# Landmark attention, gated MLP and Mish MLP: the fused weight product moved to the front, w1 and w2 reloaded as fp32, landmark evictions twice as wide

## The chip, the core and the metric

The kernel runs on one core of one Trainium2 chip. The metric is the device time in microseconds (us). Five engines work side by side, each through its own list of instructions in order: TensorE (PE; its weight loads are shown as PEld), VectorE (DVE), ScalarE (ACT), GpSimd (POOL), and SyncE (SP), which here only issues DMAs. Semaphores make an engine wait for another.

## The reference

Landmark attention (32 landmarks, 6 steps of an iterative inverse) feeds a gated MLP without activation between its weights, and that feeds an MLP with Mish:

```
q_lm, k_lm = means of q and k over 18 tokens       # batch 4, 8 heads, 576 tokens, head 64
A = softmax(q k_lm^T); Bm = softmax(q_lm k_lm^T); C = softmax(q_lm k^T)
Z = Bm^T / (norms of Bm); 6 times: Z = 2Z - Z Bm Z
x = A Z C v                                        # 2304 tokens x 512
h = (x w1) * (x w2);  y = h w3 w_out               # w1, w2: 512 x 1024
out = (g w_out2), g = mish(y w_in)                 # w_in: 512 x 2048
```

All weights arrive as float64; q, k and v as fp32.

## The kernel before

**Decoding.** A weight unit is 128 x 512 float64 numbers, 512 KB. `ld` (SP) loads it, `da` (ACT or DVE, `top_bits`) takes the top bits, and `db` (DVE, `join`, L214) joins them with the rest into fp32. Units `wo0` to `wo7` are w_out of the gated MLP, `w30` to `w315` are w3 transposed, `w{bp}{s}{x}` are 16 units of w1 and w2, and 32 numbered units are the Mish MLP's weights.

**Stages.** (1) `mm n x` multiplies w3 by w_out once for all tokens, since no activation stands between them: 64 fp32 products, which PE runs as 128 instructions (L344). (2) Attention for batches 0 to 3 (names with the batch last): sums over 18 tokens, scores, softmaxes, the inverse's six steps (`nm`, `nu`), and a landmark matrix `LT`. `A` is not multiplied out: it stays as two halves high and low (`ahi`, `alo`) of the operand `AT`. (3) `m b s` multiplies LT of a batch by w1 and w2 (L784, 8 fp32 products, which PE runs as 16 instructions). The result is evicted from PSUM as a high part (`mh`, ACT) and a low part (`ml`, DVE, `less`, L223) into one of three slots `M`. `xa` and `xb` multiply AT by a slot for w1 and w2, six products each (a pair of high and low parts takes three: L194 to L196); `xc` (ACT) and `xm` (DVE) make the gated product, `sh` and `sl` split it. (4) `y` multiplies it by the result of (1). (5) The Mish MLP runs in 24 steps, each of products `Z` and then `O`; the first of its products, `Z0 0`, ends what the text calls the first part of the program.

Batches 0 and 1 take w1 and w2 in a first pass (`bp` 0), 2 and 3 in a second (`bp` 1); before the change each pass loads and decodes all 16 units.

**What sets the order.** Each step is recorded with its engine, what it must follow and which buffers it takes. The table `ORDER` then says in what order the steps are issued; `issue` goes through it and hands out buffers from pools as their last readers pass. So an engine's list is the table's, and a table entry such as `da w34@ACT` also sets the engine. Twenty products of a tile of ones (`SPIN`) run on PE before the first step.

PSUM has eight banks, all in one pool `w`. An `m` takes two of them, one for each of two head groups, and is evicted in four pieces of 128 x 256 a kind.

Of the kernel before, what the change touches and what calls it, by code (L numbers as in the profile page):

```python
# [223 lines left out]

# [1231 lines left out]
```

## Time and profile before

| | |
|---|---|
| time, 3 runs | 717.61 us (717.41 to 718.4) |
| profiled execution, its own time | 719.34 us |
| its span, first to last instruction | 717.5 us |
| busy: PE, DVE, ACT, POOL | 702.5, 419.1, 287.3, 11.2 us |
| instructions on PE (products) | 5004 |
| bytes moved by DMA | 141.38 MB, mean 197 GB/s |
| chain that ended last | PE 94%, DMA 2%, DVE 2%, ACT 1% |

The profiled execution took 719.34 us, 1.73 us more than the median of the runs. Busy time is the time in which an engine had an instruction under way. Matmuls are pipelined, so that their busy times overlap and are longer than what each adds: 302 ns busy for one of 128 x 288 where one starts every 132 ns. The work that a stretch holds is therefore counted in starts and not in busy time. `PEclk` is the clock that TensorE was granted, 1.00 for 2.4 GHz and 0.50 for 1.2 GHz.

### The profile page before, as it was taken

What the parts mean: (1) busy time and instruction counts of PE and PEld (TensorE: products, weight loads), DVE (VectorE), ACT (ScalarE), POOL (GpSimd) and SP (SyncE); (2) the same over time, 40 slices, a digit from 0 to 9 for tenths busy, and PEclk for the clock granted to TensorE, in tenths of its full rate; (3) what the DMA queues carried; (4) which work ended last, traced back from release to release, by engine and by line L of the source; (5) the groups of instructions that cost most, each with busy time, mean ns of one, the idle gap of its engine ahead of it and who ended that gap; (6) DMA issues with size and microseconds to landing.
All of it is one profiled execution on the core that took longest, in us unless ns stands there. A gap on an engine that the chain in (4) does not pass through costs nothing.

```text
span 717.5 us, 12433 instructions
## 1 busy us (share of the span) xinstructions
PE 702.5 (98%) x5004; PEld 597.5 (83%) x5004; DVE 419.1 (58%) x904; ACT 287.3 (40%) x649; POOL 11.2 (2%) x13
## 2 busy tenths in 40 slices
...
GB/s 337 318 289 242 240 206 248 108 194 148 60 89 89 90 134 219 146 207 252 315 65 220 221 350 194 291 232 248 272 211 209 163 205 206 180 219 208 171 1 88
DMA packets 33914, 141.38 MB, mean 197 GB/s; under 512 B 3392, under 2 KB 3776, under 8 KB 30272
## 3 DMA queue, kind: packets, MB, share of 16 engines
...
HBM read 110.69 MB, written 29.88 MB: 196 GB/s over the span
## 4 chain that ended last, share of the span: by engine, by line
PE 94%; DMA 2%; DVE 2%; ACT 1%; issue 0%; SPq 0%; ACTq 0%; DVEq 0%
PE ps L194 27%; PE ps L195 27%; PE ps L196 27%; PE ps L344 7%; PE ps L784 2%; DMA raw<-in_wts_dram 2%; PE ps L405 1%; PE ps L597 1%; DMA q<-in_qT_dram 1%; PE ps L531 1%; PE ps L510 0%; DVE e L420 0%; DVE cmx L481 0%; DVE mx L426 0%; DVE ea L463 0%
## 5 line engine op out<-in xcount | busy, mean ns | idle before, releaser
L195 PE MATMUL ps<-hs,W 128*128 128x288 f32 (+1 forms) x298 | 92.3, 310 | 0.0
L194 PE MATMUL ps<-hs,W 128*128 128x288 f32 (+1 forms) x298 | 92.3, 310 | 0.0
L196 PE MATMUL ps<-hs,W 128*128 128x288 f32 (+1 forms) x298 | 92.2, 309 | 0.0
L1254 DVE TENSOR_TENSOR hsb<-ps,zt 128x384 f32<-128x384 f32 x72 | 39.7, 556 | 88.7 <-PE ps L196 88.2
L1250 ACT ACTIVATE hsb<-hsb 128x768 f32<-128x768 f32 (+1 forms) x48 | 32.8, 684 | 117.4 <-DVE hsb L1254 117.4
L194 PE MATMUL ps<-AT,M 128*128 128x288 f32 x256 | 77.4, 302 | 0.0
L196 PE MATMUL ps<-AT,M 128*128 128x288 f32 x256 | 75.5, 295 | 0.0
L195 PE MATMUL ps<-AT,M 128*128 128x288 f32 x256 | 75.4, 294 | 0.0
L1254 DVE TENSOR_TENSOR zt<-ps,zt 128x384 f32<-128x384 f32 x48 | 26.7, 556 | 83.1 <-PE ps L196 81.0
L344 PE MATMUL ps<-wo,raw 128*128 128x512 f32 x128 | 60.6, 616 | 1.3 <-DVE wo L214 1.3
L194 PEld LDWEIGHTS ps<-hs,W 128*128 128x128 f32 x298 | 56.0, 188 | 2.1 <-ACT M L218 0.8
L196 PEld LDWEIGHTS ps<-hs,W 128*128 128x128 f32 x298 | 55.9, 188 | 1.8
L195 PEld LDWEIGHTS ps<-hs,W 128*128 128x128 f32 x298 | 56.1, 188 | 1.3
L223 DVE TENSOR_TENSOR W<-hsb,W 128x384 fp32r<-128x384 f32 (+1 forms) x72 | 48.8, 686 | 9.6 <-ACT W L1251 9.5
L194 PEld LDWEIGHTS ps<-AT,M 128*128 128x128 f32 x256 | 48.0, 188 | 5.1 <-issue 2.6
L195 PEld LDWEIGHTS ps<-AT,M 128*128 128x128 f32 x256 | 48.1, 188 | 0.5 <-issue 0.5
L196 PEld LDWEIGHTS ps<-AT,M 128*128 128x128 f32 x256 | 48.0, 188 | 0.0
L344 PEld LDWEIGHTS ps<-wo,raw 128*128 128x128 f32 x128 | 24.3, 200 | 26.4 <-issue 21.1
L218 ACT ACTIVATE a<-ps 128x288 f32<-128x288 f32 x64 | 25.5, 411 | 50.9 <-PE ps L196 46.3
L202 ACT ACTIVATE top<-raw 128x512 f16<-128x512 bf16 x48 | 37.3, 785 | 8.8 <-DMA raw<-in_wts_dram 6.2
L195 PE MATMUL ps<-yH,zw 128*128 128x384 f32 x120 | 40.3, 336 | 0.1
L195 PE MATMUL ps<-yH,hs 128*128 128x384 f32 x120 | 40.2, 335 | 0.0
...
## 6 DMA issues: line engine op xcount, KB each, us to landing
...
```

Source lines behind the costliest of these rows:

```text
L194: T.matmul(out=o, lhsT=lh, rhs=rh, start=first, stop=False, skip_group_check=partial)
L195: T.matmul(out=o, lhsT=lh, rhs=rl, start=False, stop=False, skip_group_check=partial)
L196: T.matmul(out=o, lhsT=ll, rhs=rh, start=False, stop=last, skip_group_check=partial)
L202: S.activation(o, i, ACTF.Copy)
L218: S.activation(o, x, ACTF.Copy)
L223: (G if e == "POOL" else V).tensor_tensor(o, x, f32(hi), op=ALU.subtract)
L344: T.matmul(out=got(f"acc{i}"), lhsT=f32(middle(got(f"w3{n}"))[:, o:o + 128]), rhs=WO0[j // 4][:, j % 4], start=j == 0, stop=j == 7)
L405: T.matmul(out=mine(f"{key}{g}{hf}")[32 * i:32 * i + 32, 0:HALF], lhsT=st[lm][r, p, :], rhs=st[x][r, p, hf * HALF:(hf + 1) * HALF], start= ...
L531: T.matmul(out=pc[32 * i:32 * i + 32, :], lhsT=et[0:w, ck, 32 * i:32 * i + 32], rhs=VT[0:w, ck, h * D:(h + 1) * D], start=(ck == 0), stop= ...
L784: T.matmul(out=got(f"p{c}{key}")[32 * i:32 * i + 32], lhsT=LT[r, b, 2 * c + par, :], rhs=w12(f"w{bp}{s}{2 * c + par}")[r], start=True, sto ...
L1250: S.activation(e, src_, ACTF.Mish)
L1254: V.tensor_tensor(o, x, y, op=ALU.add)
```

## The change

Nothing of PE's arithmetic changes: both kernels have 4258 products in their tables' order (5004 as the trace counts them). What changes:

1. **Order.** `ORDER` is a new table. It begins with the units of w_out and w3 and their products; q and k of batch 0 are loaded behind eight weight units, and attention stands between the products.
2. **w1 and w2** are decoded once, stored to DRAM as fp32 (`wsm`, 256 KB each) and loaded from there for the second pass. 16 loads of 512 KB and 16 decodes go; 16 stores and 16 loads of 256 KB come. Both make 8.4 MB.
3. **Evictions of `m`.** Two of the eight PSUM banks become one tile `PAIR` of two banks. Attention of batches 0 and 1 uses them first (pool `v`), then every `m` uses `PAIR` (pool `m2`, one entry), and after the last `m` they return to `w` as two banks. An `m` is now evicted in two pieces of 128 x 512 a kind, where it was four of 128 x 256.
4. **Small operations of attention** move: the softmax of `Bm` takes its shift, exponent and sum in ACT instructions, some additions go to ACT, and POOL takes the subtraction of the row maximum (`asb`, 7 of 8) and the low half of `AT` (`alo`, 6 of 8).

```diff
 ORDER = (
-    "lk0 0,lq0 0,lq1 0,ks3 0,qs3 0,qs4 0,lk1 0,cs0 0,ks4 0,cm00 0,cs1 0,cm10 0,lk0 1,bs 0,cm20 0,cex00 0,ks3 1,"
+    "ld wo0,da wo0@ACT,db wo0,ld w34,da w34@DVE,ld w30,da w30@ACT,db w34,db w30,mm 0 1,ld wo1,da wo1@DVE,db wo1,"
...
-    bank = [ps.tile([128, 512], F32, name=f"ps{i}") for i in range(8)]
+    bank = [ps.tile([128, 512], F32, name=f"ps{i}") for i in range(6)]
+    PAIR = ps.tile([128, 2, 512], F32, name="pair")
+    bank += [PAIR[:, 0], PAIR[:, 1]]
...
-    pools["w"] = bank[0:8]
+    pools["w"], pools["v"], pools["m2"] = bank[0:6], bank[6:8], []
...
-            add(f"asb{g}", "DVE", [f"amx{g}"], a_sub(g))
+            add(f"asb{g}", ("DVE", "POOL"), [f"amx{g}"], a_sub(g))
...
-            add(f"alo{g}", "DVE", [f"ahi{g}"], a_out(g, 1), (), (), [f"ea{g}"])
+            add(f"alo{g}", ("DVE", "POOL"), [f"ahi{g}"], a_out(g, 1), (), (), [f"ea{g}"])
...
+        if bp:
+            step(f"ld {u}", "SP", [f"wsm {d}"], lambda e: nc.sync.dma_start(out=w12(u), in_=WMD[d * 128:(d + 1) * 128, :]),
+                 {"f" + u: "w12"})
+            return
         decode(u, 24 + 4 * s + x, lambda: got(u), {u: "raw"}, lambda: w12(u), ([], {"f" + u: "w12"}, [u]))
+        step(f"wsm {d}", "SP", [f"db {u}"], lambda e: nc.sync.dma_start(out=WMD[d * 128:(d + 1) * 128, :], in_=w12(u)), (), ["f" + u])
...
-                p, m = got(f"p{c}{key}")[:, 256 * x:256 * x + 256], mslot(b, 2 * s + x)
+                p, m = got("p" + key)[:, :, 256 * x:256 * x + 256], mslot(b, 2 * s + x)
                 if i == 0:
-                    copy(e, m[:, 0, c], p)
+                    copy(e, m[:, 0], p)
                 else:
-                    less(e, m[:, 1, c], p, m[:, 0, c])
+                    less(e, m[:, 1], p, m[:, 0])
...
-            for c in range(2):
-                step(f"mh{c} {n}", "ACT", [key, f"mt {n}"], ev(0, c, x))
-                step(f"ml{c} {n}", "DVE", [f"mh{c} {n}"], ev(1, c, x), (), [f"p{c}{key}"])
+            step(f"mh {n}", "ACT", [key] + vacated, ev(0, x), {f"M {n}": "M"})
+            step(f"ml {n}", "DVE", [f"mh {n}"], ev(1, x), (), ["p" + key])
```

SP's list at the start of the program, before and then after (`raw` is the landing place of a weight unit, `k` and `q` are halves of a batch):

```order
L257 DMA idn<-in_ident_dram 128x128
L381 DMA k<-in_kT_dram 128x2x576
L381 DMA q<-in_qT_dram 128x2x576 x2
L381 DMA k<-in_kT_dram 128x2x576
L381 DMA k_72<-in_kT_dram 128x2x576 x2
L210 DMA raw_73<-in_wts_dram 128x2048
L381 DMA q_71<-in_qT_dram 128x2x576 x2
L210 DMA raw_73<-in_wts_dram 128x2048
```

```order
L260 DMA idn<-in_ident_dram 128x128
L202 DMA raw_73<-in_wts_dram 128x2048 x3
L202 DMA raw<-in_wts_dram 128x2048 x4
L202 DMA raw_73<-in_wts_dram 128x2048
L384 DMA k<-in_kT_dram 128x2x576 x2
L384 DMA q<-in_qT_dram 128x2x576 x2
L202 DMA raw_73<-in_wts_dram 128x2048 x3
```

Eight weight units now stand ahead of batch 0's q and k, where six halves of q and k stood ahead of the first unit.

PE's list around `m 0 2` and the first product that reads it (`xa 0 4 0`, the last row after); before, `m 0 2` ends with ps_77 and ps_82, and the rows with ps_79 and ps_83 are `m 1 2`, behind which 16 score products stand:

```order
L784 MATMUL ps_77<-w_669,LT 32x512
L784 MATMUL ps_82<-w_669,LT 32x512
L784 MATMUL ps_79<-w_669,LT 32x512
L784 MATMUL ps_83<-w_805,LT 32x512
L784 MATMUL ps_79<-w_669,LT 32x512
L784 MATMUL ps_83<-w_805,LT 32x512
```

```order
L793 MATMUL pair<-w_370,LT 32x512 x8
L534 MATMUL ps_78<-vt,et 32x64 x20
L186 MATMUL ps_80<-AT_69,M 128x288
L187 MATMUL ps_80<-AT_69,M 128x288
L188 MATMUL ps_80<-AT_69,M 128x288
L186 MATMUL ps_80<-AT_69,M 128x288
L187 MATMUL ps_80<-AT_69,M 128x288
L188 MATMUL ps_80<-AT_69,M 128x288
L186 MATMUL ps_79<-AT_68,M 128x288
```

The two `m` of a pair of batches no longer follow each other, and between `m 0 2` and its first reader stand 20 products of probabilities with v (40 as the trace counts) and one block `xb`.

POOL's list from its start, before (where five more like the last row follow, and nothing else) and after (`e` is a half of A's softmax, `ea` the same turned back):

```order
L1372 MEMSET top 128x1024
L457 ISA
L457 TENSOR_TENSOR e_94<-e_94,sm 128x576
L457 TENSOR_TENSOR e_93<-e_93,sm 128x576
L457 TENSOR_TENSOR e_94<-e_94,sm 128x576
```

```order
L1384 MEMSET top 128x1024
L221 ISA
L221 TENSOR_TENSOR e_92<-e_92,mx 128x576
L221 TENSOR_TENSOR cc<-nm 128x2
L460 TENSOR_TENSOR e_92<-e_92,sm 128x576
L460 TENSOR_TENSOR e_93<-e_93,sm 128x576
L224 TENSOR_TENSOR AT_68<-ea_94,AT_68 128x576
L224 TENSOR_TENSOR AT_68<-ea_95,AT_68 128x576
L221 TENSOR_TENSOR e_93<-e_93,mx 128x576
L221 TENSOR_TENSOR e_92<-e_92,mx 128x576
```

POOL has 20 long operations instead of 8, and each kind of them reads two tiles in SBUF.

## Rows read from the trace of the kernel before

**Rows 1.** Stretches of 10 us: PE, PEld, DVE, ACT, POOL busy (x instructions), clock, DMA share, GB/s

```profile
10.00:20.00 10.00, 6.44 (x100) 2.58 (x101) 9.41 (x25) 3.29 (x9) 0.00 (x0) 0.57 1.04 394
...
60.00:70.00 10.00, 10.00 (x66) 4.07 (x65) 9.85 (x24) 7.51 (x22) 0.00 (x0) 1.00 0.76 267
```

**Rows 2.** Timeline of PE: start, length, engine, line, operation, [idle before, releaser]

```profile
1.45 6.01 PE L1376 MATMUL ps<-ones 128*128 128x512 bf16 x20 [1.45 <-DVE ones L1374]
...
18.66 0.44 PE L597 MATMUL ps<-bt 32*32 32x32 f32 x16 [2.03 <-DVE bt L592]
...
26.76 1.13 PE L344 MATMUL ps<-wo,raw 128*128 128x512 f32 x2 [1.31 <-DVE wo L214]
...
64.61 1.95 PE L784 MATMUL ps<-w,LT 64*32 64x512 f32 x32
...
336.38 0.34 PE L194 MATMUL ps<-yW,zw 128*128 128x384 f32 x1
```

**Rows 3.** The chain that ended last, several stretches: start, length, engine, line, instructions

```profile
51.87 0.83 PE ps L531 x40
52.95 0.36 PE ps L597 x16
...
64.68 1.88 PE ps L784 x32
66.56 7.07 PE ps L344 x16
...
103.18 0.97 PE ps L405 x32
...
134.20 0.44 PE ps L510 x4
134.64 0.11 PE ps L512
```

**Rows 4.** A stretch of 40 us that holds only L194 to L196

```profile
290.00:330.00 40.00, 40.00 (x303) 40.00 (x302) 30.92 (x68) 24.32 (x57) 0.00 (x0) 1.00 0.46 168
```

**Rows 5.** Timeline of DVE at the start

```profile
5.61 1.35 DVE L393 TENSOR_REDUCE sumk<-k 128x64 f32<-128x1152 f32 x1 [4.21 <-DMA k<-in_kT_dram]
...
8.63 1.35 DVE L393 TENSOR_REDUCE sumq<-q 128x64 f32<-128x1152 f32 x1 [0.15 <-DMA q<-in_qT_dram]
```

**Rows 6.** Groups of ACT and DVE by form: xcount, busy, mean ns, idle before

```profile
L202 ACT ACTIVATE top<-raw 128x512 f16<-128x512 bf16 x48 | 37.3, 785 | 8.8 <-DMA raw<-in_wts_dram 6.2 <-DVE wo L214 2.4
L214 DVE SCALAR_TENSOR_TENSOR wo<-raw,top 128x512 int32<-128x512 int32 x8 | 5.5, 683 | 0.2
```

**Rows 7.** A microsecond while PE was busy at the low clock

```profile
33.00:34.00 1.00, 1.00 (x2) 0.34 (x1) 1.00 (x3) 1.00 (x5) 0.00 (x0) 0.50 0.62 158
```

**Rows 8.** DVE's busy time until the first product of m

```profile
5.61:64.61 59.00, 50.59 (x685) 23.64 (x683) 55.85 (x140) 24.79 (x64) 5.09 (x4) 0.86 0.87 316
```

**Rows 9.** Timelines of POOL and of DVE under it

```profile
37.80 1.61 POOL L457 TENSOR_TENSOR e<-e,sm 128x576 f32<-128x576 f32 x1 [36.12 <-DVE sm L452]
...
49.67 1.16 POOL L457 TENSOR_TENSOR e<-e,sm 128x576 f32<-128x576 f32 x1 [8.22 <-ACT et L521]
...
38.80 1.16 DVE L214 SCALAR_TENSOR_TENSOR raw<-raw,top 128x512 int32<-128x512 int32 x1
...
50.17 0.69 DVE L447 TENSOR_SCALAR sm<-sm 128x18 f32<-128x18 f32 x1
```

**Rows 10.** Evictions by form, ACT and DVE

```profile
L218 ACT ACTIVATE W<-ps 128x512 fp32r<-128x512 f32 x8 | 4.8, 603 | 5.4 <-PE ps L344 5.4
L223 DVE TENSOR_TENSOR M<-ps,M 128x256 fp32r<-128x256 f32 x64 | 25.1, 417 | 8.0 <-ACT M L218 6.4 <-PE ps L196 1.1
L223 DVE TENSOR_TENSOR W<-ps,W 128x512 fp32r<-128x512 f32 x8 | 5.4, 688 | 2.5 <-ACT W L218 2.4
```

**Rows 11.** The chain where the Mish stage waited longest

```profile
460.76 0.19 PE ps L196
...
463.68 0.44 PE ps L195
```

More of the change, by code (lines that the diff above doesn't have):

```diff
@@ L220, in copy, with plus, pair @@
             (G if e == "POOL" else V).tensor_scalar(o, x, 1.0, 0.0, op0=ALU.mult, op1=ALU.add)
+    def plus(e, o, x, c):
+        if e == "ACT":
+            S.activation(o, x, ACTF.Copy, bias=c)
+        else:
+            V.tensor_scalar(o, x, c, None, op0=ALU.add)
+    def pair(e, o, x, y, op):
+        (G if e == "POOL" else V).tensor_tensor(o, x, y, op=op)
     def less(e, o, x, hi):
@@ L295, in issue @@
                     free[p].append(i)
-            for key, p in moves.get(n, ()):
-                pools[p].append(got(key))
+            for _, p, x in moves.get(n, ()):
+                pools[p].append(x)
                 free[p].append(len(pools[p]) - 1)
         assert len(done) == len(steps)
-    pools["w"] = bank[0:8]
+    pools["w"], pools["v"], pools["m2"] = bank[0:6], bank[6:8], []
     pools["raw"] = [RAW[:, 1024 * i:1024 * i + 1026] for i in range(4)]
@@ L430, in f @@
             def f(e):
-                V.tensor_tensor(by_token(g), by_token(g), st["mx", g].unsqueeze(2).to_broadcast([128, NT, L]), op=ALU.subtract)
+                pair(e, by_token(g), by_token(g), st["mx", g].unsqueeze(2).to_broadcast([128, NT, L]), ALU.subtract)
             return f
@@ L446, in f @@
             def f(e):
-                V.tensor_scalar(st["sm", g], st["sm", g], 1e-9, None, op0=ALU.add)
+                plus(e, st["sm", g], st["sm", g], 1e-9)
             return f
@@ L564, in b_max, with b_neg, b_exp, b_mul @@
             return f
-        def b_sub(g):
+        def b_neg(e):
+            st["bng"] = sbt([128, 2], "bng", 2)
+            V.tensor_scalar(st["bng"], st["bmx"], -scale / (BLK_T * BLK_T), None, op0=ALU.mult)
+        def b_exp(g):
             def f(e):
                 if g == 0:
-                    st["be"] = sbt([128, 2, L], "be", 2)
-                V.tensor_scalar(st["be"][:, g, :], st["pb"][g], st["bmx"][:, g:g + 1], None, op0=ALU.subtract)
-            return f
-        def b_exp(e):
-            S.activation(st["be"], st["be"], ACTF.Exp, scale=scale / (BLK_T * BLK_T))
-        def b_sum(e):
-            st["bsm"] = sbt([128, 2], "bsm", 2)
-            V.tensor_reduce(st["bsm"], st["be"], axis=AX.X, op=ALU.add)
+                    st["be"], st["bsm"] = sbt([128, 2, L], "be", 2), sbt([128, 2], "bsm", 2)
+                S.activation(st["be"][:, g, :], st["pb"][g], ACTF.Exp, bias=st["bng"][:, g:g + 1],
+                             scale=scale / (BLK_T * BLK_T), accum_out=st["bsm"][:, g:g + 1])
+            return f
         def b_add(e):
-            V.tensor_scalar(st["bsm"], st["bsm"], 1e-9, None, op0=ALU.add)
+            plus(e, st["bsm"], st["bsm"], 1e-9)
         def b_rec(e):
             V.reciprocal(st["bsm"], st["bsm"])
-        def b_mul(e):
-            st["bm"] = sbt([128, 2, L], "bm", 2)
-            V.tensor_tensor(st["bm"], st["be"], st["bsm"].unsqueeze(2).to_broadcast([128, 2, L]), op=ALU.mult)
+        def b_mul(g):
+            def f(e):
+                if g == 0:
+                    st["bm"], st["ns"] = sbt([128, 2, L], "bm", 2), sbt([128, 4], "ns", 2)
+                S.activation(st["bm"][:, g, :], st["be"][:, g, :], ACTF.Copy, scale=st["bsm"][:, g:g + 1],
+                             accum_out=st["ns"][:, g:g + 1])
+            return f
         def b_tr(e):
@@ L603, in b_p0, with n_sum @@
                 tile_mm(st["pp"][:, g, :], st["bt"][:, g, :], st["bt"][:, g, :])
-        def n_sum(i):
-            def f(e):
-                if i == 0:
-                    st["ns"] = sbt([128, 4], "ns", 2)
-                V.tensor_reduce(st["ns"][:, 2 * i:2 * i + 2], st["bt" if i else "bm"], axis=AX.X, op=ALU.add)
-            return f
+        def n_sum(e):
+            V.tensor_reduce(st["ns"][:, 2:4], st["bt"], axis=AX.X, op=ALU.add)
         def n_cp(e):
             st["bc"] = sbt([128, 4, L], "bc", 1)
-            V.tensor_copy(st["bc"], st["ns"].unsqueeze(2).to_broadcast([128, 4, L]))
+            copy(e, st["bc"], st["ns"].unsqueeze(2).to_broadcast([128, 4, L]))
         def n_tr(e):
@@ L625, in n_mul @@
             st["cc"] = sbt([128, 2], "cc", 2)
-            V.tensor_tensor(st["cc"], st["nm"][:, 0:2], st["nm"][:, 2:4], op=ALU.mult)
+            pair(e, st["cc"], st["nm"][:, 0:2], st["nm"][:, 2:4], ALU.mult)
         def n_add(e):
-            V.tensor_scalar(st["cc"], st["cc"], 1e-6, None, op0=ALU.add)
+            plus(e, st["cc"], st["cc"], 1e-6)
         def n_rec(e):
@@ L637, in f @@
                     st["py"] = sbt([128, 2, 2, L], "py", 2)
-                V.tensor_tensor(st["py"][:, :, i, :], st["bm" if i else "pp"],
-                                st["cc"].unsqueeze(2).to_broadcast([128, 2, L]), op=ALU.mult)
+                x = st["bm" if i else "pp"]
+                if e == "ACT":
+                    for g in range(2):
+                        S.activation(st["py"][:, g, i, :], x[:, g, :], ACTF.Copy, scale=st["cc"][:, g:g + 1])
+                else:
+                    V.tensor_tensor(st["py"][:, :, i, :], x, st["cc"].unsqueeze(2).to_broadcast([128, 2, L]), op=ALU.mult)
             return f
@@ L686, in attn @@
         for g in range(2):
-            add(f"bmx{g}", "DVE", ["bs"], b_max(g), old(2, "bsb0", "bsb1"))
+            add(f"bmx{g}", "DVE", ["bs"], b_max(g), old(2, "bng"))
+        add("bng", "DVE", ["bmx0", "bmx1"], b_neg, old(2, "by0", "by1"))
         for g in range(2):
-            add(f"bsb{g}", "DVE", [f"bmx{g}"], b_sub(g), old(2, "bml"), (), [f"pb{g}"])
-        add("by", "ACT", ["bsb0", "bsb1"], b_exp)
-        add("bsm", "DVE", ["by"], b_sum, old(2, "bml"))
-        add("bad", "DVE", ["bsm"], b_add)
+            add(f"by{g}", "ACT", ["bng"] + ["by0"] * g, b_exp(g), old(2, "bml1"), (), [f"pb{g}"])
+        add("bad", ("DVE", "ACT"), ["by0", "by1"], b_add)
         add("brc", "DVE", ["bad"], b_rec)
-        add("bml", "DVE", ["brc"], b_mul, old(2, "npy1", "ns0"))
-        add("btr", "DVE", ["bml"], b_tr, old(2, "ns1", "bp"))
+        for g in range(2):
+            add(f"bml{g}", "ACT", ["brc"] + ["bml0"] * g, b_mul(g), old(2, "npy1", "ns1", "nc"))
+        add("btr", "DVE", ["bml0", "bml1"], b_tr, old(2, "ns1", "bp"))
         add("bp", "PE", ["btr"], b_p0, (), {"pp0": "w"})
-        add("ns0", "DVE", ["bml"], n_sum(0), old(2, "nc"))
-        add("ns1", "DVE", ["btr", "ns0"], n_sum(1))
-        add("nc", "DVE", ["ns0", "ns1"], n_cp, old(1, "ntr"))
+        add("ns1", "DVE", ["btr"], n_sum)
+        add("nc", ("DVE", "ACT"), ["bml1", "ns1"], n_cp, old(1, "ntr"))
         add("ntr", "DVE", ["nc"], n_tr, old(1, "nx"))
         add("nx", "DVE", ["ntr"], n_max, old(2, "nml"))
-        add("nml", "DVE", ["nx"], n_mul, old(2, "npy0", "npy1"))
-        add("nad", "DVE", ["nml"], n_add)
+        add("nml", ("DVE", "POOL"), ["nx"], n_mul, old(2, "npy0", "npy1"))
+        add("nad", ("DVE", "ACT"), ["nml"], n_add)
         add("nrc", "DVE", ["nad"], n_rec)
-        add("npy0", "DVE", ["bp", "nrc"], b_py(0), old(2, "lt0", "lt1"), (), ["pp0"])
-        add("npy1", "DVE", ["nrc", "bml", "npy0"], b_py(1))
+        add("npy0", ("DVE", "ACT"), ["bp", "nrc"], b_py(0), old(2, "lt0", "lt1"), (), ["pp0"])
+        add("npy1", ("DVE", "ACT"), ["nrc", "bml1", "npy0"], b_py(1))
         for k in range(6):
@@ L716, in attn @@
         for hf in range(2):
-            add(f"as{hf}", "PE", [ks, "lq1"], a_scores(hf), (), {f"sc{g}{hf}": "w" for g in range(2)})
+            add(f"as{hf}", "PE", [ks, "lq1"], a_scores(hf), (), {f"sc{g}{hf}": "w" if hf or b > 1 else "v" for g in range(2)})
         for hf in range(2):
@@ L722, in attn @@
             add(f"amx{g}", "DVE", [f"at0{g}", f"at1{g}"], a_max(g), e_old(g, "asb"))
-            add(f"asb{g}", "DVE", [f"amx{g}"], a_sub(g))
+            add(f"asb{g}", ("DVE", "POOL"), [f"amx{g}"], a_sub(g))
             add(f"aex{g}", "ACT", [f"asb{g}"], a_exp(g))
             add(f"asm{g}", "DVE", [f"aex{g}"], a_sum(g), e_old(g, "amul"))
-            add(f"aad{g}", "DVE", [f"asm{g}"], a_add(g))
+            add(f"aad{g}", ("DVE", "ACT"), [f"asm{g}"], a_add(g))
             add(f"arc{g}", "DVE", [f"aad{g}"], a_rec(g))
@@ L760, in add_w12 @@
     def add_w12(bp, s, x):
-        u = f"w{bp}{s}{x}"
+        u, d = f"w{bp}{s}{x}", 4 * s + x
+        if bp:
+            step(f"ld {u}", "SP", [f"wsm {d}"], lambda e: nc.sync.dma_start(out=w12(u), in_=WMD[d * 128:(d + 1) * 128, :]),
+                 {"f" + u: "w12"})
+            return
         decode(u, 24 + 4 * s + x, lambda: got(u), {u: "raw"}, lambda: w12(u), ([], {"f" + u: "w12"}, [u]))
+        step(f"wsm {d}", "SP", [f"db {u}"], lambda e: nc.sync.dma_start(out=WMD[d * 128:(d + 1) * 128, :], in_=w12(u)), (), ["f" + u])
     def w12(u):
@@ L783, in mm, with ev @@
                     r, par = slice(64 * (h % 2), 64 * (h % 2) + 64), i // 2
-                    T.matmul(out=got(f"p{c}{key}")[32 * i:32 * i + 32], lhsT=LT[r, b, 2 * c + par, :],
+                    T.matmul(out=got("p" + key)[32 * i:32 * i + 32, c, :], lhsT=LT[r, b, 2 * c + par, :],
                              rhs=w12(f"w{bp}{s}{2 * c + par}")[r], start=True, stop=True,
                              tile_position=(64 * (h % 2), 32 * i))
-        def ev(i, c, x):
+        def ev(i, x):
             def f(e):
-                p, m = got(f"p{c}{key}")[:, 256 * x:256 * x + 256], mslot(b, 2 * s + x)
+                p, m = got("p" + key)[:, :, 256 * x:256 * x + 256], mslot(b, 2 * s + x)
                 if i == 0:
-                    copy(e, m[:, 0, c], p)
+                    copy(e, m[:, 0], p)
                 else:
-                    less(e, m[:, 1, c], p, m[:, 0, c])
+                    less(e, m[:, 1], p, m[:, 0])
             return f
-        step(key, "PE", [f"lte0 {b}", f"lte1 {b}"] + [f"db w{bp}{s}{x}" for x in range(4)]
-             + chain("m", key), mm, {"p0" + key: "w", "p1" + key: "w"}, [f"fw{bp}{s}{x}" for x in range(4)])
+        step(key, "PE", [f"lte0 {b}", f"lte1 {b}"] + [f"{'ld' if bp else 'db'} w{bp}{s}{x}" for x in range(4)]
+             + chain("m", key), mm, {"p" + key: "m2"}, [f"fw{bp}{s}{x}" for x in range(4)])
         for x in range(2):
             n = f"{b} {2 * s + x}"
-            step(f"mt {n}", "none", vacated, lambda e: None, {f"M {n}": "M"})
-            for c in range(2):
-                step(f"mh{c} {n}", "ACT", [key, f"mt {n}"], ev(0, c, x))
-                step(f"ml{c} {n}", "DVE", [f"mh{c} {n}"], ev(1, c, x), (), [f"p{c}{key}"])
+            step(f"mh {n}", "ACT", [key] + vacated, ev(0, x), {f"M {n}": "M"})
+            step(f"ml {n}", "DVE", [f"mh {n}"], ev(1, x), (), ["p" + key])
     def hslice(u, s):
@@ L827, in add_ab @@
             me = f"{x} {key}"
-            step(me, "PE", [f"ml0 {b} {s}", f"ml1 {b} {s}"] + [f"alo{g} {b}" for g in range(2)] + chain("x", me), ab(i),
+            step(me, "PE", [f"ml {b} {s}"] + [f"alo{g} {b}" for g in range(2)] + chain("x", me), ab(i),
                  {"ab"[i] + key: "w"}, [f"M {b} {s}"])
@@ L1085 @@
     in_m = [first[i - 1] for i in RAW_M]
+    step("join", "none", [f"at0{g} 1" for g in range(2)], lambda e: None, {f"v{i}": "v" for i in range(2)})
+    moves["join"] = [("v0", "m2", PAIR)]
     vacated = [f"db {u}" for u in in_m] + [f"mm {u[2:]} {i}" for u in in_m if u[1] == "3" for i in range(4)]
@@ L1113 @@
     WFD = dr.tile([256, 2048], F32, name="wfd")
+    WMD = dr.tile([2048, 512], F32, name="wmd")
     zd = [ZD[q * 128:(q + 1) * 128, :] for q in range(NQ)]
@@ L1120, in early @@
             after = [name]
+    step("split", "none", [f"ml {b} 7" for b in range(B)], lambda e: None, {"pp": "m2"})
+    moves["split"] = [("pp", "w", PAIR[:, i]) for i in range(2)]
     done_ab = [f"xb {b} 7 {h}" for b in (2, 3) for h in range(2)]
@@ L1140, in made @@
         x = x_ops(n)
-        was = [last_read[MADE[s - 4]]] if s >= 4 else [f"db w13{s}"]
+        was = [last_read[MADE[s - 4]]] if s >= 4 else [f"db w03{s}"]
         step(x[0][0], "SP", was, x[0][2], {f"x {s}": "raw"} if s < 4 else {})
```

252 rows, old and new, of the table ORDER are left out of this document.

## The prediction, made before the run

> **What bounds the kernel now.** I read the page's busy shares first: PE 98%, DVE 58%. Busy PE is not PE at its pace, so I took the pace of each kind of product from a stretch where nothing else ran and asked how much work the first part of the program, up to the first Mish product, holds. A 128 x 288 product starts every 40 us / 302 = 0.1325 us [rows 4]; 1536 of them make 203.5 us. In the chain of waits 16 fp32 instructions of the fused weight take 7.07 us, so 128 take 56.6; the 256 of m take 256/32 x 1.88 = 15.0. Attention: scores 256/32 x 0.97 = 7.8, probabilities with v 320/40 x 0.83 = 6.6, the inverse 448/16 x 0.36 = 10.1, transposes 8 x (0.44 + 0.11) = 4.4, 128 small ones about 2.2: 31.1 [rows 3]. Sum: 306.2 us.
>
> The first Mish product starts at 336.38 [rows 2], so PE lost 30.2 us before it. Where? The first m starts at 64.61 [rows 2]. PE's list ahead of it holds 48 fused instructions (21.2) and attention of two batches with a piece of the third (16.7), 37.9 in all: 26.7 us are lost by then, and only 3.5 in the 272 us after. The timeline shows why: after the spin (1.45 to 7.46) PE has next to nothing, waits 2.03 us for a small DVE result at 18.66, and gets its first fused product at 26.76 [rows 2]; from 10 to 20 us its clock is 0.57 and DVE is busy 9.41 of 10 [rows 1]. DVE is the bound there: 140 instructions and 55.85 of 59.0 us busy until the first m [rows 8].
>
> **The change, part by part.** Durations are of the profiled execution, 719.34 us; the median of the runs is 1.73 lower, and the sum is carried over as a difference. PE's instructions stay the same, so the time can only come from what PE loses, and goes through when it starts, and what it then waits for.
>
> *Start.* The first half of k landed at 5.61 and the second transfer after it let DVE go at 8.63: 1.51 us for each 576 KB [rows 5], so 1.34 for a 512 KB unit. The first unit lands at 5.61 - 0.17 = 5.44, w30, the third, at 8.12. Top bits on ACT 0.785, join on DVE 0.683 [rows 6], about 0.1 for a semaphore: first product at 9.7. (If the three land together, it is the same 9.7.) Ends: 9.0 and 11.0. After that eight units are in at 14.8 and q and k of batch 0 at 20.9; the 13 products of these units keep PE until 9.7 + 13 x 0.884 = 21.2. The next product needs w32 and wo4 (23.6) joined behind four sums and four transposes on DVE, and the next small result (btr) a chain over ACT: about 0.5 us of waiting each, 1.0 in all (0 to 3).
>
> *Clock.* Idle from 7.46 to 9.7, PE may be granted the low clock as it was at 33 us, where it was busy and still at 0.50 [rows 7]; that spell lasted 3.4 us and cost half of it. I take 1.0 (0 to 1.7).
>
> *DVE.* In the new list, too, 139 DVE instructions stand ahead of the first m, but 11 joins and 6 low halves of the fused weight more (0.685 instead of the mean 59.0/140 = 0.42: +4.5) and two sums of 1.35 more (+1.9). DVE starts at 6.2, waits some 4.4 for loads until 25, and is ready at 6.2 + 4.4 + 58.8 + 6.4 = 75.8 (58.8 is the 59.0 without the handoff to PE). PE's list ahead of m holds all 128 fused instructions (56.6) and 15.1 of attention: 9.7 + 71.7 + 2.0 = 83.4. For the second m, 85.0 stand against 89.1. So DVE is ahead by 4 to 8 us, and POOL's share eats from that: a join took 1.16 instead of 0.68 while POOL ran, and an addition of 128 x 18 took 0.69, both ending with or just after POOL's operation, which itself took 1.61 instead of 1.16 when it met a DVE instruction [rows 9]. Ten long POOL operations stand ahead of the second m, six more than before: 6 x 0.47 = 2.8 of the 4.1. I take 1.5 us of waiting for PE (0 to 5.6; the upper end if each of the ten holds DVE for its whole 1.16: 11.6 - 1.9 - 4.1).
>
> The Trainium skill, "SBUF — State Buffer", section "Who interferes with whom", says that a DVE instruction with two SBUF inputs and a GpSimd instruction that reads SBUF exclude each other, and the second waits for the whole of the first; it speaks against giving POOL `asb` and `alo`. By that rule the worst case is the 5.6 just given; the rows agree with it, at 0.47 a meeting.
>
> *Evictions.* A piece of 128 x 512 costs 0.603 on ACT and 0.688 on DVE where two of 128 x 256 cost 2 x 0.417 on DVE [rows 10]: DVE saves 32 x 0.146 = 4.7 us over all, off the path. On the path is the delay from an m to its first reader: 0.603 + 0.688 and three handoffs of 0.2 make 1.9. Before, m of two batches stood together and covered each other: the smallest cover was 2.0. Now, PE's work between an m and its first reader, priced as above, is 1.59, 1.62, 1.86, 1.91, four times 2.39, 2.94 and seven times 3.2 to 8.0. With nothing ahead on ACT and DVE that costs 0.6, with one operation ahead on each (DVE's mean of 0.42 for both) 5.4. I take 2.0, nearer to the lower end: in a stretch of the middle ACT was busy 24 of 40 us and DVE 31 [rows 4], so that an eviction finds its engine free, or soon free, more often than not.
>
> *Decoding once.* 16 joins and 16 top bits go, and the bytes stay as they were. No second-pass unit was on the chain; this is worth nothing by itself, but DVE gets slack behind 90 us. A store makes SP wait for its join, and the next loads behind it (units for the m after next, 15 us ahead) wait with it: 0.
>
> *Mish stage.* Same work in another order; its largest loss, 460.95 to 463.68, is 2.73 [rows 11]. 0 (-2.7 to +3).
>
> Sum: before 26.7, after 9.7 + 1.0 + 1.0 + 1.5 + 2.0 = 15.2; -11.5 us. 719.34 - 11.5 = 707.8 for a profiled execution, 717.61 - 11.5 = 706.1 for the median.
>
> **Rivals.**
> - *Weights come too slowly.* DMA gave 394 GB/s from 10 to 20 us, but 267 from 60 to 70 at a share of 0.76 [rows 1]. At 267 a unit takes 1.96 us: first product 11.0, PE waits 5.5 for q at 28.0 and 1.7 for wo4: 8.5 more, 1.0 of which is in the sum: 713.6. Against: 0.76 is a queue that had not always work; at the start it has.
> - *Evictions in a queue, slower than before.* One PAIR and in-order lists: if 2.5 operations stand ahead of each piece on ACT and DVE, the delay is 1.9 + 2.5 x 0.84 = 4.0, and 11 of 16 covers fall short, by 17.7 us: 717.61 - 26.7 + 13.2 + 17.7 = 721.8. It decides from two ahead (13.1: 717.2). For: DVE was busy 9.85 of 10 us from 60 to 70 [rows 1]. Against: the new DVE list is shorter behind the first m, by the second decodes, `asb` and `alo`.
> - *No new wait at all*, and the Mish stage loses its 2.73: 717.61 - 17.0 - 2.7 = 697.9. For: PE lost only 3.5 in 272 us before. Against: DVE and PE stand 4 us apart over 80 us.
> - *The first products start no earlier* (the loads land late, or PE waits for a third engine) would leave the order without effect: no row speaks for it, as k landed at 5.61.
>
> **How the numbers follow.** Forecast 0.68 (702 to 711), slow weights 0.12, evictions in a queue 0.10, no wait 0.10. Leaving out a tenth at either end gives 700 to 714. 0.2% of the time is 1.4 us, about what a measurement of this kernel can tell from no change. Faster: 0.68 + 0.12 + 0.10 less a little of the slow weights, 0.88; within 0.2%, 0.04, from between two cases; slower 0.08, from the third.
>
> **What would show it.** The first L347 row on PE at 9 to 11 us and the first L793 row at 81 to 86 (before 64.61, but with all fused products behind it); the first Mish product at 324 to 327; PE's clock back at 1.00 before 20 us; joins of over 1 us only under POOL's rows; PE idle before its first product behind an m under 0.5 us in most cases. Wrong, if PE waits more than 5 us between 10 and 60, or if DVE is the releaser of PE for more than 8 us before 140.

## The result, and the profile after

The changed kernel takes 709.65 us (six runs, 708.93 to 712.96) against 717.7 us for the kernel before (six runs, 717.41 to 718.98): a ratio of 0.9891 with a 95% interval of 0.9871 to 0.9912, 8.05 us less. The forecast was 706.1 us in a range of 700 to 714. The profiled execution of the changed kernel took 709.42 us, close to its median, with a span of 707.6 us.

The answer to [rows 2] first. The timeline of PE after the change (start, length, engine, line, operation; in brackets the idle time ahead and its releaser; L347 is the fused weight, L793 is m, L186 opens the Mish stage):

```profile
1.45 6.05 PE L1388 MATMUL pair<-ones 128*128 128x512 bf16 x20 [1.45 <-DVE ones L1386]
9.22 11.43 PE L347 MATMUL ps<-wo,raw 128*128 128x512 f32 x26 [1.71 <-DVE raw L206]
...
82.04 1.09 PE L793 MATMUL pair<-w,LT 64*32 64x512 f32 x16
...
324.88 0.34 PE L186 MATMUL ps<-yW,zw 128*128 128x384 f32 x1
```

The first fused product starts at 9.22 (before: 26.76), the first m at 82.04, the first Mish product at 324.88: 11.50 us ahead of 336.38. So against that one execution of the kernel before, the whole forecast of 11.5 us is there by the end of the first part; against a second one it is 10.0 (the last experiment). Stretches of the changed kernel answer to [rows 1, 8] (columns as there), and two cover the rest of the first part and the Mish stage; the last row is the kernel before's Mish stage, from its own trace:

```profile
10.00:20.00 10.00, 10.00 (x24) 4.52 (x23) 8.44 (x12) 0.00 (x0) 0.00 (x0) 1.00 1.04 401
...
9.22:82.00 72.78, 72.78 (x668) 34.49 (x668) 66.27 (x144) 30.35 (x85) 14.08 (x12) 1.00 0.92 323
...
82.00:324.88 242.88, 241.59 (x2453) 219.58 (x2445) 154.58 (x352) 114.22 (x299) 12.54 (x10) 1.00 0.45 155
324.88:707.60 382.72, 376.65 (x1874) 337.57 (x1872) 171.12 (x315) 134.07 (x257) 0.00 (x0) 1.00 0.54 203
```

```profile
336.38:717.50 381.12, 376.22 (x1874) 337.57 (x1872) 172.96 (x316) 134.25 (x256) 0.00 (x0) 1.00 0.54 205
```

The clock is 1.00 throughout. From 9.22 to 82.0 PE is busy for 72.78 of 72.78 us, although DVE still is for 66.27: DVE is nearly as full as before, but PE no longer hangs on it. The Mish stage takes 382.72 us where it took 381.12: 1.60 us are given back there. The view of all that PE waits for in the changed kernel (us in total, times, longest) has seven rows:

```profile
PE ps L347 <- DVE raw L206: 1.7, 1, 1.7
PE pair L1388 <- DVE ones L1386: 1.5, 1, 1.5
PE pair L186 <- ACT hsb L1243: 1.4, 2, 0.7
PE ps L186 <- DVE hsb L1266: 0.7, 1, 0.7
PE pair L793 <- DVE M L224: 0.5, 2, 0.3
PE pair L186 <- ACT y L210: 0.5, 1, 0.5
PE ps L187 <- DVE yH L224: 0.3, 1, 0.3
```

The first two are the start. Of the five others three have PE as writer of `pair`. The two of 0.7 us behind ACT's `hsb` are in the Mish stage, where no m is left. This is the first of them, PE and then ACT:

```profile
571.78 0.40 PE L188 MATMUL pair<-wy,W 128*128 128x512 f32 x1
572.87 0.50 PE L186 MATMUL pair<-wy,W 128*128 128x512 f32 x1 [0.69 <-ACT hsb L1243]
```

```profile
572.22 0.60 ACT L1243 ACTIVATE hsb<-pair 128x512 f32<-128x512 f32 x1 [1.37 <-PE pair L188]
```

By the pools, `ob0` and `ob1` got the two halves of PAIR. ACT copies `ob0` out, and PE's product into `ob1`, the other bank, starts only when that copy ends. The Trainium skill, "PSUM — Partial Sum Buffer", section "PSUM bank collisions raise a hardware error", asks for a guard by bank and quadrant; these are two banks, so what would order them is that the program made one tile of them. The next experiments test that.

### The profile page after: what moved, and what is told of

The parts are those of the page before. It is cut to its first block, busy times and chain, and to the rows that moved or that the text cites. A ratio compares the mean times of both kernels' runs of the same rounds, so it can differ in the third digit from the quotient of the medians.

```text
span 707.6 us, 12346 instructions
## 1 busy us (share of the span) xinstructions
PE 697.1 (99%) x5004; PEld 593.9 (84%) x5004; DVE 395.0 (56%) x814; ACT 281.5 (40%) x644; POOL 27.8 (4%) x27
## 4 chain that ended last, share of the span: by engine, by line
PE 96%; ACT 1%; DVE 1%; DMA 1%; issue 0%; SPq 0%; ACTq 0%
PE ps L186 23%; PE ps L187 23%; PE ps L188 23%; PE ps L347 8%; PE pair L186 4%; PE pair L188 4%; PE pair L187 4%; PE pair L793 2%; PE ps L602 1%; PE ps L408 1%; PE ps L534 1%; DMA raw<-in_wts_dram 1%; PE ps L513 1%; ACT M L210 0%; DVE M L224 0%
## 5 line engine op out<-in xcount | busy, mean ns | idle before, releaser
L186 PE MATMUL ps<-AT,M 128*128 128x288 f32 x256 | 77.8, 304 | 0.1
L187 PE MATMUL ps<-hs,W 128*128 128x288 f32 (+1 forms) x236 | 72.6, 308 | 0.0
L186 PE MATMUL ps<-hs,W 128*128 128x288 f32 (+1 forms) x236 | 72.6, 308 | 0.0
L188 PE MATMUL ps<-hs,W 128*128 128x288 f32 (+1 forms) x236 | 72.5, 307 | 0.0
L347 PE MATMUL ps<-wo,raw 128*128 128x512 f32 x128 | 58.6, 604 | 1.7 <-DVE raw L206 1.7
L224 DVE TENSOR_TENSOR W<-hsb,W 128x384 fp32r<-128x384 f32 (+1 forms) x72 | 49.1, 685 | 17.4 <-ACT W L1263 17.4
L186 PEld LDWEIGHTS ps<-AT,M 128*128 128x128 f32 x256 | 48.0, 188 | 9.5 <-issue 5.0
L347 PEld LDWEIGHTS ps<-wo,raw 128*128 128x128 f32 x128 | 24.0, 196 | 27.4 <-issue 20.7
L188 PEld LDWEIGHTS ps<-hs,W 128*128 128x128 f32 x236 | 44.3, 188 | 1.2
L187 PEld LDWEIGHTS ps<-hs,W 128*128 128x128 f32 x236 | 44.5, 188 | 1.0
L186 PEld LDWEIGHTS ps<-hs,W 128*128 128x128 f32 x236 | 44.3, 188 | 1.0
L210 ACT ACTIVATE a<-ps 128x288 f32<-128x288 f32 x64 | 25.6, 410 | 45.7 <-PE ps L188 44.5
L831 DVE TENSOR_TENSOR h<-a,ps 128x288 f32<-128x288 f32 x64 | 28.0, 449 | 26.0 <-ACT hs L210 9.7
```

Source lines behind the costliest of these rows:

```text
L186: T.matmul(out=o, lhsT=lh, rhs=rh, start=first, stop=False, skip_group_check=partial)
L187: T.matmul(out=o, lhsT=lh, rhs=rl, start=False, stop=False, skip_group_check=partial)
L188: T.matmul(out=o, lhsT=ll, rhs=rh, start=False, stop=last, skip_group_check=partial)
L347: T.matmul(out=got(f"acc{i}"), lhsT=f32(middle(got(f"w3{n}"))[:, o:o + 128]), rhs=WO0[j // 4][:, j % 4], start=j == 0, stop=j == 7)
L831: V.tensor_tensor(hslice(u, s), got("s" + key), got("b" + key)[:, 0:HALF], op=ALU.mult)
```

## The experiments

All times are medians, but for "A change of kind, 64 times" and "The kernel before, traced again", which are one run each. The kernel before stood at 717.84 to 717.93 us beside them. Differences are to the yardstick, the first of these runs.

**The changed kernel again**, as the yardstick.

> The changed kernel as it is, so that the three kernels beside it have their yardstick on the same chip. Theory (half of a tile): products into one half of PAIR wait for ACT's copy out of the other half, because both halves are one tile; so the three stops of PE at 318.4, 572.9 and 698.1 us (0.66, 0.86 and 0.85 us) stand at the same places again. Rival (chance): they are delays of this one execution and lie elsewhere now. Both: 709.0 to 710.5 us.

709.93 us, ratio 0.9896 [0.988, 0.9913]. The stops stand at 318.1, 572.6 and 697.9 us with the same lengths: not chance.

**Halves of PAIR kept apart, by order and banks.**

```diff
-    ...,ye 7 1,...,y 7 2,...
+    ...,y 7 2,ye 7 1,...
-            takes = {..., "O0 0": ["ob0", "ob1", "ob2"], ...
+            takes = {..., "O0 0": ["ob0", "ob2", "ob1"], ...
```

> The changed kernel, with the two halves of PAIR kept apart where a product followed an eviction of the other half: ob1 and ob2 change banks, and y 7 2 is issued ahead of the eviction of y 7 1. No instruction is added or removed. Theory (half of a tile): the three stops of 0.66, 0.86 and 0.85 us go, 2.4 us less than the changed kernel: about 707.3 us. Rival (the stop is ACT's): what PE waits for is ACT being late with these copies, whatever bank they come from; then other banks wait as long, and the time stays within 0.5 us of the changed kernel's.

709.0 us. Its profiled execution has a span of 705.8 us, 1.6 below the 707.4 of the yardstick. All three stops are gone, and a new one came:

```profile
326.94 0.44 PE L187 MATMUL ps<-yW,zw 128*128 128x384 f32 x1 [0.72 <-DVE yW L224]
```

By the changed order, the eviction of `y 7 1` came later and DVE's `yW` with it. So the expectation of 707.3 failed on the median (its four runs lie between 707.6 and 710.2), though its mechanism held; the next kernel leaves the order alone.

**The same by banks alone.**

```diff
+            if n == "y 7 2":
+                free["w"][0:2] = free["w"][1::-1]
...
-            takes = {..., "O0 0": ["ob0", "ob1", "ob2"], ...
+            takes = {..., "O0 0": ["ob0", "ob2", "ob1"], ...
```

> The changed kernel, with the halves of PAIR kept apart by banks alone: ob1 and ob2 change banks, y 7 2 and y 7 3 change banks, and no engine's order changes (in the kernel before this one the eviction of y 7 1 came later, and a low half on DVE with it: a new stop of 0.98 us at 326.9). Theory (half of a tile): all three stops of 0.66, 0.86 and 0.85 us go and none comes: the first Mish product at 324.0, span 705.0, median about 707.5 us against 709.9. Rival (something else is late behind the first stop, as at 326.9): only the two of the last stage go, 1.7 us: 708.2 us.

707.62 us, ratio 0.9857 [0.9842, 0.9872]: 2.3 us below the yardstick, as the three stops make it, and the best but one of all kernels here. PE's waits have neither `hsb L1243` nor `y L210` any more:

```profile
PE ps L349 <- DVE raw L206: 1.1, 1, 1.1
PE ps L410 <- ACT M L210: 0.9, 1, 0.9
PE ps L186 <- DVE hsb L1268: 0.7, 1, 0.7
PE pair L795 <- DVE M L224: 0.5, 2, 0.3
PE ps L187 <- DVE yH L224: 0.3, 1, 0.3
```

The row of 0.9 (at 85.4 us) is in no other trace; with it and a first product 0.3 us later, this one execution's first Mish product was at 325.67 and not at 324.0, and its time, 708.16, was among the slower of its runs. ACT was idle for 1.13, 1.37 and 3.18 us ahead of the three copies in the changed kernel, and the stops went when only banks moved: the rival of the run before (ACT is late) falls.

**q and k first.** The four loads of batch 0's q and k go ahead of `ld wo0`; nothing else.

```diff
-    "ld wo0,da wo0@ACT,db wo0,ld w34,...
+    "lk0 0,lk1 0,lq0 0,lq1 0,ld wo0,da wo0@ACT,db wo0,ld w34,...
...
```

> The changed kernel, with the four loads of batch 0's q and k put ahead of the first weight unit; nothing else moves. Theory (the early start is the gain): the first unit lands 4 x 1.51 = 6.0 us later, so the first fused product starts at 15.3 instead of 9.3, and PE, which has nothing else ahead of it in its list, loses 6.0 us, and half of any stretch at the low clock after so long an idle time (0 to 7): 716 to 723 us. Rival (DVE's list sets the pace whatever is loaded first): PE catches up behind 25 us, since sums, scores and turns come earlier: 709 to 712 us.

718.03 us, ratio 1.0001: this one edit takes the whole gain back.

```profile
15.48 2.07 PE L347 MATMUL ps<-wo,raw 128*128 128x512 f32 x2 [8.12 <-DVE raw L206]
```

```profile
10.00:15.00 5.00, 0.00 (x0) 0.00 (x0) 2.02 (x4) 1.55 (x2) 0.00 (x0) 0.62 1.03 410
15.00:20.00 5.00, 4.52 (x6) 1.94 (x7) 4.04 (x9) 0.00 (x0) 0.00 (x0) 0.50 0.84 334
20.00:22.00 2.00, 2.00 (x5) 0.82 (x4) 1.97 (x4) 0.00 (x0) 0.00 (x0) 0.64 0.00 0
22.00:30.00 8.00, 8.00 (x27) 3.48 (x33) 4.64 (x4) 1.56 (x2) 0.00 (x0) 1.00 0.49 155
```

The first product starts 6.2 us later than in the yardstick (9.32), and after 8.12 idle us PE is at the low clock until about 21: some 6 us of work at half speed, 3 us. Together 9; the two traced executions lie 9.0 us apart (spans 716.4 and 707.4), the medians 8.1. DVE, which gets q and k sooner, gives nothing back in the trace.

**No products of ones.** `SPIN = 20` becomes `SPIN = 0`.

> The changed kernel without the 20 products of ones (SPIN = 0). Theory (clock): PE comes idle to its first fused product at 9.3 us and is granted the low clock for a stretch, as the kernel before was from about 10.9 to 24.5 us; over 7 to 14 us at half speed it loses 3.5 to 7 us: 713 to 717 us. Rival (the clock hangs on the work that follows): fused products keep PE busy from the start, so that it is granted full speed at once or after a few microseconds: 709.5 to 712 us.

712.06 us, 2.1 us more: the rival is nearer. PE's first product starts at 9.54, and its first four starts are 1.01, 0.86, 0.85 and 0.52 us apart, where 0.43 is usual in the same trace: about 1.5 us at half speed, and then full speed. The clock column says 1.00 there, so at the very beginning the text goes by the distances of starts.

**POOL's operations back on DVE.** 13 table entries, such as

```diff
-asb0 0@POOL
+asb0 0@DVE
```

> The changed kernel, with the 13 subtractions asb and low halves alo given back from POOL to DVE. Theory (start alone): DVE is ahead of PE by some microseconds in the first 90 us, so that 13 operations of about 0.7 us (9 us over 130 us of time) cost PE at most 1.5 us: 709 to 711 us. Rival (POOL carries the gain): without POOL's share DVE is the bound again until the second m, and the 9 us less the 4 to 8 us of its lead come back: 711 to 715 us. Third possibility, the shared access of DVE and POOL was what held DVE: up to 1.5 us faster than the changed kernel.

712.62 us, ratio 0.9927 [0.9915, 0.994]: 2.7 us slower, inside the rival's range. Each operation is 0.74 us on DVE and 1.24 to 1.48 on the mean on POOL, and yet POOL's are cheaper, since PE now waits for DVE:

```profile
PE ps L346 <- DVE raw L205: 1.9, 1, 1.9
...
PE pair L792 <- DVE M L223: 0.8, 3, 0.3
PE ps L407 <- DVE W L223: 0.8, 1, 0.8
...
PE ps L187 <- DVE M L223: 0.5, 1, 0.5
```

The first row is the start (1.65 in the yardstick's trace). The three others are 1.6 us more than there, without what runs out on PE ahead of each stop.

**Evictions in quarters.**

```diff
-                p, m = got("p" + key)[:, :, 256 * x:256 * x + 256], mslot(b, 2 * s + x)
+                for c in range(2):
+                    p, m = got("p" + key)[:, c, 256 * x:256 * x + 256], mslot(b, 2 * s + x)
...
```

> The changed kernel, with each m evicted from PAIR in four pieces of 128 x 256 a kind, as before, where it is two of 128 x 512. DVE gets 32 x 0.146 = 4.7 us more in all, ACT something like it, and the bank is free again about as late (0.35 + 4 x 0.42 = 2.0 us for one and 0.60 + 2 x 0.69 = 2.0 for the other). Theory (start alone): no difference, within 1 us of the changed kernel. Rival (the width pays): each of the 16 m costs its readers 0.15 to 0.3 us more, 2.4 to 5 us slower.

710.62 us, 0.7 more than the yardstick: within the expectation of no difference, with 1.0 us instead of 0.5 that m waits for DVE (`PE pair L793 <- DVE M L224`, twice in both traces). The yardstick's own five runs lie between 709.15 and 712.94, so that a worth of the width is not shown; it is a microsecond at most.

**Decoding work back in the second pass, in the way of m.** For each second-pass unit

```diff
+            step(f"da {u}", ("ACT", "DVE"), [f"ld {u}"], lambda e: again_top(e, w12(u), got("u" + u)), {"u" + u: "u"})
+            step(f"db {u}", "DVE", [f"da {u}"], lambda e: again(w12(u).bitcast(I32)), (), ["u" + u])
```

and m waits for `db`. `again_top` takes the top bits of the reloaded unit, `again` is an OR of it with itself.

> The changed kernel, with the work of decoding put back into the second pass: after each of the 16 reloads of 256 KB, top bits (8 on ACT, 8 on DVE) of that unit and an OR of 128 x 512 that leaves the numbers as they are; m waits for it. Stores and loads stay. Theory (decoding once is worth nothing): DVE gets 16 x 0.69 + 8 x about 0.6 = 16 us between 135 and 235 us, where it has slack: within 1 us of the changed kernel. Rival (DVE's slack is used up, as it was when the 13 operations came back from POOL and cost 2.7 us): 2 to 5 us slower, 712 to 715 us.

725.24 us, 15.3 us slower, beyond both theories. The main wait (8.2 us in three stops) is m behind `again`:

```profile
195.94 1.10 PE L808 MATMUL pair<-w,LT 64*32 64x512 f32 x7 [4.61 <-DVE w L768]
```

In the new table a reload stands as little as one entry ahead of its m, so a decode in between is on the path. The stops cost clock as well: PE runs at the low level behind the two longest (2.3 us, then 4.6):

```profile
162.85:168.50 5.65, 5.65 (x44) 3.92 (x45) 2.07 (x3) 2.32 (x8) 0.65 (x1) 0.51 0.01 3
195.94:199.20 3.26, 3.26 (x20) 1.60 (x21) 1.13 (x2) 0.60 (x1) 0.00 (x0) 0.52 0.00 0
```

Half of these 8.9 us is another 4.4 of the 15.3. This shows what the place costs, not what the work costs; hence the next.

**The same work, and nothing waits for it.** The steps stand where they stood, but work on a scratch tile (`got("u" + u)`), and m waits for `ld` as in the changed kernel.

> The changed kernel, with the instructions of 16 decodes put into the second pass where the kernel decode_again had them (8 top bits on ACT, 8 on DVE, 16 ORs of 128 x 512 on DVE), but on a scratch tile and with no product waiting for them. Theory (the way, not the work): decode_again's 15.4 us came from decodes between a reload and its m; without that wait 16 us of DVE's time between 150 and 245 us cost at most 2 us: 709.5 to 712 us. Rival (the work): DVE is late in this stretch with its low halves of m and its gated products, and most of the 15 us come again: 718 us or more.

715.73 us, ratio 0.997: 5.8 us slower. Neither theory: with the work where it stands here, it costs two fifths of the 15.3, and waiting for it cost three fifths, the clock included. DVE is 61.7 of 95 us busy from 150 to 245 instead of 50.6, and yet PE waits for low halves and copies queued behind the extra operations. One stop cost twice:

```profile
163.00:165.00 2.00, 0.10 (x2) 0.02 (x1) 1.34 (x3) 1.07 (x6) 0.00 (x0) 1.00 0.00 0
165.00:169.00 4.00, 4.00 (x25) 2.06 (x26) 2.13 (x3) 1.74 (x6) 1.43 (x1) 0.57 0.00 0
169.00:173.00 4.00, 4.00 (x33) 4.00 (x32) 2.80 (x6) 4.00 (x12) 0.00 (x0) 1.00 0.84 283
```

PE had nothing for 1.9 us, and then ran 4 us at a clock of 0.57: 1.7 us more in this execution, which took 716.55 us. Only three of the eight runs show a mean clock under 1.00 (0.998), so in most runs the 5.8 is work and waits.

**A change of kind, 64 times.**

```diff
+    tiny = cst.tile([128, 64], F32, name="tiny")
...
+                if i == 0:
+                    T.matmul(out=got("a" + key)[0:32, HALF:HALF + 64], lhsT=tiny[0:32, 0:32], rhs=tiny[0:32], start=True,
+                             stop=True, tile_position=(0, 0))
```

> The changed kernel, with one fp32 product of 32 x 32 by 32 x 64 put ahead of each of the 64 blocks xa, into columns of its bank that nothing uses. Theory (a change of the kind of product costs PE): in the trace after the change, the last product of a run of 128 x 288 products takes 0.22 us to the next start instead of 0.13, and the first of the next run 0.24: 0.20 us for each way in and out, and 0.05 to 0.2 for the product itself: 64 x 0.25 to 0.4 = 16 to 26 us more, 726 to 736 us. Rival (changing is free, and the 0.1 us were waits for operands): 64 x 0.02 to 0.05 = 1.3 to 3.2 us more, 711 to 713 us.

`tiny` is a tile of ones. 732.91 us in one run, 23.0 more, 0.36 for each: the theory. PE has no wait that the yardstick lacks. One of the 64 in PE's timeline:

```profile
260.55 0.30 PE L187 MATMUL ps<-AT,M 128*128 128x288 f32 x1
260.68 0.29 PE L188 MATMUL ps<-AT,M 128*128 128x288 f32 x1
260.90 0.29 PE L828 MATMUL ps<-tiny 32*32 32x64 f32 x2
261.12 0.40 PE L186 MATMUL ps<-AT,M 128*128 128x288 f32 x1
261.36 0.29 PE L187 MATMUL ps<-AT,M 128*128 128x288 f32 x1
```

Starts 0.13 apart become 0.22 on the way out, 0.22 for the little product, 0.24 on the way in: 0.20 of the 0.42 is the change itself, with no wait in it. Whether it is the tile size, the shape or the type of the product that makes the change was not tried.

**POOL takes all 16.** As by banks alone, and `asb1 0`, `alo1 2`, `alo1 3` get `@POOL`.

> As apart2, and the last three of the 16 subtractions and low halves (asb1 0, alo1 2, alo1 3) also on POOL. Taking 13 back cost 2.7 us, 0.2 each. Theory (DVE's early lead is what POOL pays for): the one at 40 us may give 0 to 0.5 us, the two others none: 707.0 to 707.7 us. Rival (POOL's longer operation is on the path): a softmax half comes 0.5 to 1 us later, 707.8 to 709 us.

707.53 us, ratio 0.9855 [0.9842, 0.9869]: the same as by banks alone, within the runs' spread.

**The kernel before, traced again.**

> The kernel before, once more with its trace. Its profiled execution took 719.34 us, 1.7 us above the median of its runs; the changed kernel's was 0.2 us below its own. Theory (the base was slow): this trace has a span of about 715.9 us, with its first Mish product about 1 to 1.7 us ahead of the 336.38 of the first trace: then so much of the distance between forecast and result was in the base. Rival (the profiled execution is always so much longer): 717.5 us again, and 336.4.

717.81 us, span 716.0, first Mish product at 334.90: the theory. The stretch from 30 to 40 us, in the first trace and in this one:

```profile
30.00:40.00 10.00, 9.35 (x162) 4.87 (x163) 8.52 (x30) 5.45 (x12) 1.61 (x1) 0.83 0.83 281
```

```profile
30.00:40.00 10.00, 10.00 (x169) 5.29 (x168) 9.86 (x34) 6.42 (x15) 2.77 (x2) 0.98 0.88 319
```

The second spell at the low clock, 3.4 us in the first trace, is not there in this one. But the first spell lies elsewhere too, with about the same length: from 11.4 to 25.1 us in the first trace, from 16.8 to 30.4 in this one, as the clock from 15 to 30 us shows (first trace, then this one):

```profile
15.00:30.00 15.00, 9.99 (x128) 4.87 (x121) 14.61 (x43) 6.59 (x19) 0.00 (x0) 0.66 0.93 333
```

```profile
15.00:30.00 15.00, 9.64 (x118) 5.03 (x117) 14.65 (x43) 6.40 (x17) 0.00 (x0) 0.56 0.96 341
```

Half of 3.4 us is 1.7, and the two first Mish products are 1.5 us apart.

## Why the prediction was right, and where its sum was not

**The bound and the start: right.** The prediction said that PE loses its time before the first m because DVE feeds it, and that products of the fused weight can fill it. Putting back only the four loads cost 8.1 us, as much as the whole gain of 8.05. The first product came at 9.22 for 9.7.

**Early waits (1.0) and clock (1.0): nothing.** From 9.22 on PE stops for no wait until 122.3, and its clock never falls: it stayed at 1.00 through 1.7 idle us behind the products of ones, and fell during 8.1 (q and k first). Without the products of ones, the start paid 1.5 us.

**DVE and POOL (1.5): nothing in the first 90 us.** DVE was ahead, as worked out, and what meetings of the two engines cost did not reach PE. The rule on shared ports that the prediction drew from the Trainium skill, "SBUF — State Buffer", section "Who interferes with whom", shows in the trace where they met. This join began under a subtraction on POOL and ended 0.55 us behind it:

```profile
114.30 1.21 POOL L221 TENSOR_TENSOR e<-e,mx 128x576 f32<-128x576 f32 x1 [8.13 <-DVE mx L429]
...
114.57 1.49 DVE L206 SCALAR_TENSOR_TENSOR w<-raw,top 128x512 int32<-128x512 int32 x1
```

```profile
L206 DVE SCALAR_TENSOR_TENSOR raw<-raw,top 128x512 int32<-128x512 int32 x32 | 21.9, 685 | 2.1 <-ACT top L194 1.8
```

```profile
L224 POOL TENSOR_TENSOR AT<-ea,AT x6: 1428/1432/1621, 50.0 to 162.7; 128x576 fp32r<-128x576 f32 x6
```

It took 1.49 us where the 32 joins into `raw` have a mean of 0.685. But few meet: of the 20 long POOL operations, three took over a tenth longer than the shortest of their kind (1.66 and 1.47 for 1.16, and one `alo` 1.62 for 1.43; the last row has shortest, median and longest). The prediction had 0.47 for each of six.

**Evictions (2.0): 4, and not for the reason given.** Their own times were as priced (means of 0.597 on ACT and 0.682 on DVE, [rows 10]: 603 and 688 ns), but not the handoffs: the prediction put three of 0.2 us on the path and no row behind them. An m, ACT's copy and DVE's low half show 0.10 and 0.03:

```profile
158.52 1.09 PE L793 MATMUL pair<-w,LT 64*32 64x512 f32 x16
...
159.71 0.60 ACT L210 ACTIVATE M<-pair 128x512 fp32r<-128x512 f32 x1 [0.70 <-PE pair L793]
...
160.34 0.69 DVE L224 TENSOR_TENSOR M<-pair,M 128x512 fp32r<-128x512 f32 x1 [0.85 <-ACT M L210]
```

The first low half is done 1.42 to 1.48 us after the m in seven of the 16, where the prediction's delay to the reader was 1.9 and its smallest cover 1.59. In the trace no reader waits for `M` itself. Waits around the evictions made 1.1 us: two m that wait for PAIR (0.4 and 0.5 with what runs out ahead of them), which the prediction's term, made of readers, did not hold, and one reader (0.3, at 161.8) that waits for ACT's copy of `LT`, which stands in ACT's list behind an eviction.

What the prediction overlooked is that PE pays for each change of the kind of product. The 1536 products of 128 x 288, taken from start to start, add up to 209.8 us after and 207.0 before (203.5 by the prediction's pace), the 256 of m to 16.2 and 14.9: an m between other products pays alone what two next to each other shared, and there are 20 runs of 128 x 288 products instead of 12. Of these 4.0 us, 1.1 are the waits and 0.7 is a stop at the halves of PAIR (at 318.4, below); 2.2 are left for the changes. Another 2.0 us are products that the prediction priced too low (fused weight 57.3 for 56.6, attention 32.4 for 31.1, added up in the same way). So the sum of 15.2 came out to a tenth, from 9.2 + 4.0 + 2.0 instead of 9.7 + 1.0 + 1.0 + 1.5 + 2.0. The start was right; that the other terms came to the same was luck.

**Decoding once (0): wrong as a price in the new order.** In the order before, no second-pass unit was late. In the new order the same work on DVE and ACT, at the places where it was put, costs 5.8 us even where nothing waits for it; that each m now stands alone with less cover would explain it, and is argued, not shown. POOL's share is worth 2.7 there. These prices, and the 8.1 of the start, are of taking one part out of the changed kernel. They add up to twice the gain, so they are not shares of it: the early start comes through only with the others beside it. What each part gives in the kernel before was not run.

**Mish stage (0): +1.6.** Two of the three stops at the halves of PAIR are there, 0.86 and 0.85 us from start to start beyond the pace; the third, 0.66, is the one at 318.4. The prediction took PAIR's return "as two banks" at its word. Its lower end of -2.7 was a misreading as well: the chain in [rows 11] runs from 460.95 to 463.68 over ACT and DVE, but PE was working beside it, as a stretch of the kernel before shows:

```profile
460.00:463.00 3.00, 3.00 (x18) 2.76 (x17) 0.33 (x1) 2.11 (x4) 0.00 (x0) 1.00 0.97 416
```

**The 3.45 us between the gain forecast (11.5) and measured (8.05)** are then 1.6 of the Mish stage and 1.5 of the base: the sum was made on an execution with a second spell at the low clock, [rows 7], which the later execution, at 717.81 us like the median of the runs, did not have. Some 0.4 is left, less than the runs of one kernel differ.

**The rivals.** Slow weights: no; DMA gave 401 GB/s from 10 to 20 us, and PE did not wait. Evictions in a queue: no; 1.1 us of waits where 17.7 were priced. No new wait: nearly so before the first Mish product, but the changes of kind and PAIR took its place. Products no earlier: no.

What stays open is why one execution of the kernel with banks apart waited 0.9 us for ACT at 85.4.
